# Two conversion steps kept out of the way of a fence copy, and one transfer issued earlier

## The chip, the core and the metric

The kernel runs on one core of a Trainium2 chip. A core has a matrix engine (TensorE, PE in the profile; PEld is its weight load), a vector engine (VectorE, DVE), a scalar engine (ScalarE, ACT), GpSimd (POOL) and SyncE (SP), which here only issues DMA transfers. Each engine works through its own list of instructions; semaphores make one wait for another. The metric is the device time of one execution in microseconds, the median of several runs. Less is better.

## The reference

A retention block feeds a feed-forward block. For each of 8 batches and 8 heads the first computes decayed scores and multiplies them with v; its output, laid out as 4608 tokens by 512 features, goes through a feed-forward layer with a squared relu and 2048 hidden features.

```python
scores = scale * np.matmul(q, k.transpose(0, 1, 3, 2))        # q, k, v: (8, 8, 576, 64) float32
Dmat = np.where(rel >= 0, gamma[:, None, None] ** rel[None, :, :], 0.0)
attn = np.matmul(scores * Dmat[None, :, :, :], v)
x = attn.transpose(0, 2, 1, 3).reshape(B * S, H * D)          # (4608, 512)
h = np.maximum(x @ w_in, 0.0)                                 # w_in: (512, 2048) float64
out = (h * h @ w_out).astype(np.float32)                      # w_out: (2048, 512) float64
```

The weights arrive in double precision. The kernel turns them into float32 on the chip with integer operations on their bits.

## The kernel before

The work runs in two phases. In the first, the retention runs over chunks of 128 tokens and the first half of the feed-forward layer (x times w_in, relu, square; the result is called g) runs between its parts, block by block of 512 tokens. g is stored to DRAM. In the second phase g is loaded again and multiplied with w_out. The matrix products of blocks 1 to 8, and those of the second phase, use a scheme with seven products in place of eight, so that sums of operands are made on VectorE.

One chunk of the retention has three parts that write the same two banks of PSUM ("x's banks"). Between the second and the third stands a copy on ScalarE that reads one column of both banks and whose value is never used. It is the fence: the third part's matmuls write these banks and so wait for the copy, and the copy waits for the second part's.

```python
def retain_b(i):                       # the state of earlier chunks times q
    ...
            nc.tensor.matmul(x_at(hp, b, h), lhsT=u[rows(e), hp, :], rhs=...)                # L455
    nc.scalar.copy(u_sb[(2 * ci + (cs // CH)) % 3][:, 0:2, 0:1], xp[0][:, :, cs - CH:cs - CH + 1])   # L458

def retain_c(i):                       # scores times v, within the chunk (matmuls: L420)
    ...
```

The order of a chunk from the fifth on; `turn` transposes q and k, `scores` makes the scores, `ffn(i, half)` runs steps of the feed-forward block:

```python
retain_a(i - 1)
if i < N_CH: turn(i)
ffn(i - 1, 0)
retain_b(i - 1)                        # ends with the fence copy
if i < N_CH: scores(i)
retain_c(i - 1)
ffn(i - 1, 1)
```

A piece of a weight is converted in steps. Two of them run on ScalarE, as a pair, on 128x512 elements:

```python
def beside():
    nc.scalar.activation(exp, exp, AF.Relu, bias=exp_bias[:, 0:1], scale=2.0 ** 23)   # L213
    nc.scalar.activation(frac, lo, AF.Copy, scale=2.0 ** -52)                         # L214
```

Steps `one` (L205), `two` (L209), `three` (L217), `four` (L220) and `five` (L223) are VectorE's. The pieces of w_in are converted during the first block (`convert(6)` takes six of these steps, one piece). Those of w_out are converted during the later blocks: each step of a block (`ffn_in`) takes one part from the generator `w_out_parts`, in which `two` and `beside` are one part; sums and stores to DRAM follow the pieces.

In the first block a step is `first_in`: four matmuls (L541) and a relu of their result on ScalarE (L545), then a square on VectorE (L548). `ffn` before the change:

```python
def ffn(i, half):
    gone[0] += ...
    if steps and steps[0][0] == 0:     # the first block
        step()
        convert(6)
        if half and steps and steps[0][0] == 0:
            step()
            convert(6)
        return
    ...                                # want: where the blocks should stand by now
    if steps:
        step()
    while steps and done[0] < int(want):
        step()
```

In the later blocks a step is `ffn_in`: four matmuls (L576) and the evacuation of a bank by ScalarE (L586, L592) or VectorE (L588 to L602).

The last block's steps run after the retention has ended; between them the loads of the second phase are issued:

```python
while steps:
    n, f, *args = steps[0]
    if n == N_BLK - 1:
        if n_last in (0, 5, 10):
            fetch_g(n_last // 5)               # transfers 0, 1, 2 of g
        if n_last in (2, 9, 16, 23):
            fetch_w2(2 + n_last // 7)          # converted w_out, 1792 KB each
        ...
        n_last += 1
    step()
some(len(queue))
fetch_w2(NP - 1)
fetch_g(3)                                     # transfer 3 of g, 1024 KB
for k in range(N_K + 1):                       # the second phase, matmuls: L800
    ...
    fetch_g(k + 4)
```

Transfers 0 to 3 go to four buffers of their own (`a`), 4 and 5 to parts of a buffer that the first phase uses (`room`).

Of the kernel before, what the change touches and what calls it, by code (L numbers as in the profile page):

```python
# [40 lines left out]
def kernel(  # L41
# [147 lines left out]
    def fetch_w(j):  # L189
        if j < len(pieces) and wide:  # L190
            nc.sync.dma_start(raw_of(j).bitcast(I64).rearrange("p (c f) -> p c f", c=N_DM), piece_src(j))
# [4 lines left out]
    def round_parts(j):  # L196
        words = raw_of(j).bitcast(U32).rearrange("p (n two) -> p n two", two=2)
        lo, hi = words[:, :, 0], words[:, :, 1]
        frac = raw_of(j).rearrange("p (n two) -> p n two", two=2)[:, :, 0]
        exp = exp_of(j).bitcast(U32)  # L200
        t = piece_dst(j)
        bits = t.bitcast(U32)

        def one():
            nc.vector.tensor_scalar(exp, hi, 20, 0x7FF, op0=ALU.logical_shift_right, op1=ALU.bitwise_and)  # L205

        def two():

            nc.vector.tensor_scalar(bits, as_dst(j, hi), 0xFFFFF, 0x100000, op0=ALU.bitwise_and, op1=ALU.bitwise_or)  # L209
# [6 lines that stand above are left out]
        def three():  # L216
            nc.vector.scalar_tensor_tensor(t, bits, 2.0 ** -20, as_dst(j, frac), op0=ALU.mult, op1=ALU.add)  # L217

        def four():
            nc.vector.tensor_tensor(t, t, as_dst(j, exp_of(j)), op=ALU.mult)  # L220

        def five():
            nc.vector.scalar_tensor_tensor(bits, as_dst(j, hi), 0x80000000, bits, op0=ALU.bitwise_and, op1=ALU.bitwise_or)  # L223

        if not wide:
            to = t if pieces[j][0] == 0 else t.rearrange("p o s f -> p (o s) f")
            return [lambda: nc.sync.dma_start(to, piece_src(j))] + [lambda: None] * 5
        return [one, two, beside, three, four, five]
# [16 lines left out]
    def w_out_parts():  # L245

        for j in range(N_W1, N_W1 + 3):
            yield lambda j=j: fetch_w(j)
        for j in range(N_W1, len(pieces)):
            one, two, beside, three, four, five = round_parts(j)  # L250
            yield one
            yield lambda two=two, beside=beside: (two(), beside())
            yield three
            yield four

            def last(j=j, five=five):
                five()
                fetch_w(j + 3)

            yield last  # L260
            wi, m, e = pieces[j]
            mh, mq = divmod(m, N_MQ)
            if e == 1:

                at = slice(2 * mh, 2 * mh + 2)
                b = [stage[0][:, o, at, :] for o in range(4)] + [stage[1][:, o, at, :] for o in range(3)]
                r1, r2, r3, r4 = right_sums(*b)
                yield lambda r1=r1, r2=r2: (r1(), r2())
                yield lambda r3=r3, r4=r4: (r3(), r4())
            if e == 1 and mh == 1:  # L270

                for st_, at in ((stage[0], slice(0, 4)), (stage[1], slice(4, 7))):
                    yield from right_sums(*(st_[:, :, o, :] for o in range(NP)))
                    yield lambda st_=st_, at=at, mq=mq: nc.sync.dma_start(
                        w2_dram[at, :, mq, :].rearrange("o p f -> p o f"), st_.rearrange("p o s f -> p o (s f)"))
# [33 lines left out]
    def convert(count):  # L309
        for _ in range(count):  # L310
            f = next(w_in_steps, None)
            f and f()
# [197 lines left out]
    def g_of(mp):  # L510
        return {name: g_room[mp % 2][:, s, :, :] for s, name in enumerate(G_ORDER)}
# [16 lines left out]
    def some(count=1):  # L528
        for f in queue[:count]:
            f and f()  # L530
        del queue[:count]
# [29 lines left out]
    def ffn_in(n, mp, j):  # L561

        if j == 0 and mp == 0:

            if n not in sums_x:
                sums_x[n] = sum_x(n)
            for f in sums_x[n]:
                f()
        left, right, to = PRODUCTS[j]
        if j in OPENS:  # L570
            sums[to] = ps_f.tile([128, 2, HT], F32, tag="f", name=f"h_{to}")
        p = sums[to]
        for mm in range(2):
            w = w_in[mp][:, mm, WI_SLOT[left], :, :]
            for c in range(2):
                nc.tensor.matmul(p[:, mm, :], lhsT=w[:, c, :], rhs=xs[n][right][:, c, :],  # L576
                                 start=(j in OPENS and mm == 0 and c == 0), stop=(j in CLOSES and c == 1),
                                 skip_group_check=True)
        g = g_of(mp)
        p1, u2, p15 = (p_room[mp % 2][:, s, :, :] for s in range(3))  # L580

        def square(t):
            nc.vector.scalar_tensor_tensor(t, t, 0.0, t, op0=ALU.max, op1=ALU.mult)  # L583

        if j == 0:
            nc.scalar.copy(p1, p)  # L586
        elif j == 1:
            nc.vector.tensor_tensor(u2, p, p1, op=ALU.add)  # L588
        elif j == 2:
            nc.vector.tensor_tensor(p15, p, p1, op=ALU.add)  # L590
        elif j == 3:
            nc.scalar.activation(g["A11"], p, AF.Relu)  # L592
            nc.gpsimd.tensor_tensor(g["A11"], g["A11"], g["A11"], op=ALU.mult)  # L593
        elif j == 4:
            nc.vector.tensor_tensor(g["A22"], p, p15, op=ALU.add)  # L595
            square(g["A22"])
        elif j == 5:

            nc.vector.tensor_tensor(g["S3"], p, u2, op=ALU.add)
            square(g["S3"])  # L600
        else:
            nc.vector.tensor_tensor(g["A12"], p, p1, op=ALU.add)  # L602
            square(g["A12"])
            queue.extend(g_sums(n, mp))

        if mp == N_MP - 1 and j in (3, 4, 5) and n_next[0] > n + 1:
            if n + 1 not in sums_x:
                sums_x[n + 1] = sum_x(n + 1)
            sums_x[n + 1].pop(0)()
        if j in (6, 0, 1, 2, 3):  # L610
            some(2 if n == 1 and mp == 0 else 1)
        if n == 1 and 1 <= j < 5 and mp + 1 < N_MP:
            sums_w.setdefault(mp + 1, sum_w_in(mp + 1)).pop(0)()

        if n >= 3 or n_w2[0] < 3 + 2 * 5:
            n_w2[0] += 1
            f = next(w_out_steps, None)
            f and f()
            if n == N_BLK - 2 and (mp, j) in ((2, 3), (3, 3)):
                assert f is None  # L620
                fetch_w2(mp - 2)

    steps = []
    w_out_steps = w_out_parts()
    n_w2 = [0]

    def block_steps(n):
# [4 lines left out]
    def step():  # L634
        n, f, *args = steps.pop(0)
        done[0] += 1
        f(*args)
# [9 lines left out]
    done = [0]  # L647
# [3 lines left out]
    def ffn(i, half):  # L651

        gone[0] += chunks[max(0, min(i, N_CH - 1))][3] / 2
        if steps and steps[0][0] == 0:
            step()
            convert(6)
            if half and steps and steps[0][0] == 0:
                step()
                convert(6)
            return  # L660
        if not behind:
            behind.append((gone[0] - HALF, done[0]))
        points = behind + [p for p in PACE if p[0] > behind[0][0]]
        want = points[-1][1]
        for (x0, y0), (x1, y1) in zip(points, points[1:]):
            if gone[0] < x1:
                want = y0 + (y1 - y0) * (gone[0] - x0) / (x1 - x0)
                break
        if steps:
            step()  # L670
        while steps and done[0] < int(want):
            step()

    turn(0)
    for i in range(N_CH + 1):
# [57 lines left out]
    def fetch_g(k):  # L733
        if k < N_K:
            nc.sync.dma_start(A(k), g_dram[BLOCKS[k // NP], k % NP, :, :, :])
# [99 lines left out]
    n_last = 0  # L835
    while steps:
        n, f, *args = steps[0]
        if n == N_BLK - 1:
            if n_last in (0, 5, 10):
                fetch_g(n_last // 5)  # L840
            if n_last in (2, 9, 16, 23):
                fetch_w2(2 + n_last // 7)
            if n_last == N_MP * NP - 5:
                for f in inner_sums(0):
                    f()
            n_last += 1
        step()
    some(len(queue))
    fetch_w2(NP - 1)
    fetch_g(3)  # L850
    steps_0 = sums_0()
    for k in range(N_K + 1):
        assert k + 4 < N_K - NP or next(steps_0, None) is None
# [3 lines left out]
        for e in range(3):  # L857
# [8 lines left out]
            f = next(steps_0, None)  # L866
# [53 lines left out]
```

## Time and profile before

| | before |
|---|---|
| time, median of 3 runs | 1009.67 us (1004.35 to 1010.14) |
| span of the profiled execution | 1004.7 us |
| copies of L458 | 40, 133 to 168 ns each |
| L213, 128x512 | 32, 722 ns each (median) |
| L214, 128x512 | 32, 662 ns each (median) |
| transfers of g to `a` | 43, 1024 KB, 7.1 us from issue to landing (median) |

The page has the engines' busy shares and the span cut in 40 slices, in which a digit is the busy share of a slice in tenths:

```profile
## 2 busy tenths in 40 slices
PE   6999999999999999999999998999999999999998
...
DVE  1678797667878888798885776877677677777765
ACT  2344331122222222312311000000000000000000
...
DMA  8974665664786877579566989674764757556351
```

The first phase fills the first 24 slices or so, the second phase the rest. Other views list, for each engine, what it waited for and how long, and the instructions in order of time with the idle time ahead of each. A row such as "PE x L1 <- ACT y L2: 3.0, 5, 1.0" means that PE's instruction of line 1 was released by ScalarE's instruction of line 2 in 5 cases after 3.0 us of idle time in all, 1.0 us at the longest.

### The profile page before, as it was taken

How to read it: one execution, taken by the hardware profiler on the slowest of the kernel's cores; microseconds unless marked ns; L12 is line 12 of the kernel's file. 1: busy time of each engine (PE TensorE's matmuls, PEld its weight loads, DVE VectorE, ACT ScalarE, POOL GpSimd, SP SyncE). 2: the span in 40 equal slices, each digit the busy share in tenths (PEclk: the TensorE clock that was granted, in tenths of full speed). 3: DMA queues.
4: the chain of work that ended last, by engine and by line, in shares of the span. 5: the costliest groups of instructions: out<-in, count | busy, mean ns of one | idle time of the engine just before them, and what ended most of it. 6: DMA issues, size and time to landing. Idle time of an engine off the chain costs nothing.

```text
span 1004.7 us, 24101 instructions
## 1 busy us (share of the span) xinstructions
PE 975.3 (97%) x10376; PEld 862.4 (86%) x10376; DVE 749.7 (75%) x1418; ACT 188.9 (19%) x459; POOL 81.8 (8%) x82
## 2 busy tenths in 40 slices
PE   6999999999999999999999998999999999999998
PEld 4544688888888888788888888999999999999997
DVE  1678797667878888798885776877677677777765
ACT  2344331122222222312311000000000000000000
POOL 1200011011111111111021000000000000000000
PEclk9999999999999999999999999999999999999999
DMA  8974665664786877579566989674764757556351
GB/s 201 241 212 143 183 180 177 171 195 151 207 291 203 239 259 228 139 258 282 150 243 249 401 351 350 252 273 168 252 237 162 273 189 272 187 212 217 119 210 43
DMA packets 187658, 220.34 MB, mean 219 GB/s; under 512 B 119200, under 2 KB 137632, under 8 KB 178592
## 3 DMA queue, kind: packets, MB, share of 16 engines
q1 hardware_dynamic: 187552, 218.81, 66.8%
q8 instruction: 81, 1.33, 0.5%
q14 instruction: 25, 0.20, 0.1%
HBM read 129.39 MB, written 89.39 MB: 218 GB/s over the span
## 4 chain that ended last, share of the span: by engine, by line
PE 87%; DVE 7%; DMA 2%; ACT 2%; SPq 2%; issue 1%; DVEq 0%
PE o_b L800 16%; PE h_b L576 15%; PE o_c L800 11%; PE o_a L800 11%; PE h_a L576 10%; PE h_c L576 9%; PE h_ps L541 6%; PE x_ps L420 3%; PE t_ps L373 2%; PE x_ps L455 2%; DMA a<-g_dram 1%; PE sc_ps L399 1%; DVE room L583 1%; SPq L142 1%; DMA k_ld<-in_k_dram 1%
## 5 line engine op out<-in xcount | busy, mean ns | idle before, releaser
L576 PE MATMUL h_b<-room,w 128*128 128x256 f32 x736 | 177.3, 384 | 1.8 <-DVE room L504 1.2
L576 PEld LDWEIGHTS h_b<-room,w 128*128 128x128 f32 x736 | 137.1, 190 | 22.4 <-DVE room L595 1.4
L800 PE MATMUL o_b<-w,room 128*128 128x128 f32 x1168 | 144.5, 275 | 0.2 <-DVE room L751 0.2
L800 PEld LDWEIGHTS o_b<-w,room 128*128 128x128 f32 x1168 | 137.2, 192 | 0.5 <-DVE room L751 0.4
L800 PE MATMUL o_c<-w,room 128*128 128x128 f32 x1008 | 123.0, 275 | 0.0
L800 PEld LDWEIGHTS o_c<-w,room 128*128 128x128 f32 x1008 | 117.7, 192 | 0.0
L576 PE MATMUL h_c<-room,w 128*128 128x256 f32 x480 | 114.3, 381 | 0.0
L576 PE MATMUL h_a<-room,w 128*128 128x256 f32 x448 | 107.5, 383 | 0.0
L576 PEld LDWEIGHTS h_c<-room,w 128*128 128x128 f32 x480 | 90.5, 190 | 12.5
L576 PEld LDWEIGHTS h_a<-room,w 128*128 128x128 f32 x448 | 83.8, 190 | 11.8
L800 PE MATMUL o_a<-w,a 128*128 128x128 f32 x688 | 85.9, 275 | 2.7 <-DMA a<-g_dram 2.7
L800 PEld LDWEIGHTS o_a<-w,a 128*128 128x128 f32 x688 | 81.3, 192 | 2.9 <-issue 2.9
L593 POOL TENSOR_TENSOR room<-room 128x512 f32<-128x512 f32 x32 | 36.4, 1139 | 435.9 <-ACT room L592 380.7
L583 DVE SCALAR_TENSOR_TENSOR room<-room 128x512 f32<-128x512 f32 x96 | 67.4, 702 | 3.3
L811 ACT COPY r<-o_a 128x128 f32<-128x128 f32 x54 | 14.4, 266 | 276.9 <-PE o_a L800 246.3
L420 PEld LDWEIGHTS x_ps<-ret,v_ld 64*64 64x64 f32 x1152 | 42.5, 143 | 22.8 <-issue 14.1
L420 PE MATMUL x_ps<-ret,v_ld 64*64 64x64 f32 x1152 | 52.4, 234 | 9.1 <-ACT u_sb L458 9.1
L541 PE MATMUL h_ps<-room,w 128*128 128x512 f32 x128 | 59.9, 616 | 0.8 <-ACT room L477 0.7
L595 DVE TENSOR_TENSOR room<-h_b,room 128x512 f32<-128x512 f32 x32 | 22.0, 689 | 42.0 <-PE h_b L576 42.0
L408 POOL TENSOR_TENSOR v_ld<-v_ld,dv 128x512 f32<-128x512 f32 (+1 forms) x40 | 45.0, 1129 | 80.4 <-DMA v_ld<-in_v_dram 67.4
L541 PEld LDWEIGHTS h_ps<-room,w 128*128 128x128 f32 x128 | 24.0, 195 | 27.8 <-issue 25.2
L807 DVE TENSOR_TENSOR small<-o_b,small 128x128 f32<-128x128 f32 x63 | 18.3, 291 | 38.5 <-PE o_b L800 38.4
(94 smaller groups left out, 1369.4 us busy)
## 6 DMA issues: line engine op xcount, KB each, us to landing
g_dram<-room SPq DMA_DIRECT2D x32, 1792.0 KB, 8.1
a<-g_dram SPq DMA_DIRECT2D x43, 1024.0 KB, 7.1
room<-g_dram SPq DMA_DIRECT2D x20, 1024.0 KB, 6.0
w<-w_dram SPq DMA_DIRECT2D x7, 1792.0 KB, 12.1
out_dram<-room SPq DMA_DIRECT2D x18, 512.0 KB, 3.3
v_ld<-in_v_dram SPq DMA_DIRECT2D x32, 256.0 KB, 4.0
w<-in_moe_w_in_dram SPq DMA_DIRECT2D x16, 512.0 KB, 4.9
w<-in_moe_w_out_dram SPq DMA_DIRECT2D x16, 512.0 KB, 4.0
```

Source lines behind the costliest of these rows:

```text
L373: nc.tensor.transpose(p[:, h, j, hp, :], loaded[i][j][rows(h), 2 * hp:2 * hp + 2, :], ident[rows(h), rows(h)])
L408: nc.gpsimd.tensor_tensor(vs[:cs], vs[:cs], dv[:cs, :, ci:ci + 1].to_broadcast([cs, H, D]), op=ALU.mult)
L420: own.append(lambda hp=hp, e=e, b=b: nc.tensor.matmul(x_at(hp, b, h), lhsT=s["vs"][rows(h), 2 * hp + b, :], rhs=s["ret"][rows(h), e, hp, : ...
L455: nc.tensor.matmul(x_at(hp, b, h), lhsT=u[rows(e), hp, :], rhs=s["qT"][rows(e), hp, CH * h:CH * h + CH], start=clears(b, hp // 2), stop=Fa ...
L541: nc.tensor.matmul(p.rearrange("p h t -> p (h t)"), lhsT=w[:, c, :], rhs=xT[0][:, c, :], start=(c == 0), stop=(c == N_DM - 1))
L576: nc.tensor.matmul(p[:, mm, :], lhsT=w[:, c, :], rhs=xs[n][right][:, c, :], start=(j in OPENS and mm == 0 and c == 0), stop=(j in CLOSES a ...
L583: nc.vector.scalar_tensor_tensor(t, t, 0.0, t, op0=ALU.max, op1=ALU.mult)
L593: nc.gpsimd.tensor_tensor(g["A11"], g["A11"], g["A11"], op=ALU.mult)
L595: nc.vector.tensor_tensor(g["A22"], p, p15, op=ALU.add)
L800: nc.tensor.matmul(p, lhsT=s["lefts"][left][:, m, :], rhs=w_out[j][:, m, WO_SLOT[right], :], start=(i in OPENS and m == 0), stop=(i in CLO ...
L807: nc.vector.tensor_tensor(s["u2"], p, s["p1"], op=ALU.add)
L811: nc.scalar.copy(r[:, 0, 0:128], p)
```

## The change

Three things. In the first block, the first half of a chunk now runs its conversion ahead of its step, so that L213 and L214 come before the relu in ScalarE's order and not between the relu and the fence copy. In the later blocks, the last step before the fence does not take a part that holds the pair; the pair waits for the next step. And the fourth transfer of g is issued in the last block, at its sixteenth step, and no longer after it. The aim is that the fence copy finds ScalarE free, and that the fourth transfer lands before it is needed.

```diff
@@ w_out_parts
-            yield lambda two=two, beside=beside: (two(), beside())
+            yield two, beside
@@ ffn_in
         if n >= 3 or n_w2[0] < 3 + 2 * 5:
-            n_w2[0] += 1
-            f = next(w_out_steps, None)
-            f and f()
+            if not (held[0] and type(w_out_next[0]) is tuple):
+                n_w2[0] += 1
+                f = w_out_next[0]
+                w_out_next[0] = next(w_out_steps, None)
+                for f in f if type(f) is tuple else (f,):
+                    f and f()
@@ ffn
         if steps and steps[0][0] == 0:
-            step()
-            convert(6)
+
+            for f in (step, lambda: convert(6)) if half else (lambda: convert(6), step):
+                f()
@@ ffn, later blocks
-        if steps:
-            step()
-        while steps and done[0] < int(want):
-            step()
+        count = max(1, int(want) - done[0])
+        while steps and count:
+            held[0] = half == 0 and count == 1
+            step()
+            count -= 1
+        held[0] = False
@@ the last block
-            if n_last in (0, 5, 10):
+            if n_last in (0, 5, 10, 15):
                 fetch_g(n_last // 5)
@@ after it
     fetch_w2(NP - 1)
-    fetch_g(3)
```

Left out of the diff: the start values of `held` and `w_out_next`, and an assertion on the latter.

More of the change, by code (lines that the diff above doesn't have):

```diff
@@ L615, in ffn_in @@
         if n >= 3 or n_w2[0] < 3 + 2 * 5:
-            n_w2[0] += 1
-            f = next(w_out_steps, None)
-            f and f()
+            if not (held[0] and type(w_out_next[0]) is tuple):
[4 more added lines that the diff above has]
+                    f and f()
             if n == N_BLK - 2 and (mp, j) in ((2, 3), (3, 3)):
-                assert f is None
+                assert w_out_next[0] is None
                 fetch_w2(mp - 2)
@@ L626 @@
     w_out_steps = w_out_parts()
+    w_out_next = [next(w_out_steps)]
+    held = [False]
     n_w2 = [0]
```

## The prediction

> **What bounds the kernel now.** I read the page's busy shares first, then the list of what TensorE waited for, then the timeline around the longest of those waits.
>
> ```profile
> span 1004.7 us, 24101 instructions
> PE 975.3 (97%) x10376; PEld 862.4 (86%) x10376; DVE 749.7 (75%) x1418; ACT 188.9 (19%) x459; POOL 81.8 (8%) x82
> ```
>
> TensorE (PE) is busy 975.3 us of 1004.7; no other engine is near. The change neither adds nor removes a matmul, so 975.3 stays, and all that can be won lies in 1004.7 - 975.3 = 29.4 us. The list of PE's waits (engine, line, whom it waited for: us in total, times, longest) says whose they are:
>
> ```profile
> PE x_ps L420 <- ACT u_sb L458: 9.1, 13, 1.4
> PE t_ps L373 <- DMA k_ld<-in_k_dram: 4.4, 4, 3.2
> PE o_a L800 <- DMA a<-g_dram: 2.7, 1, 2.7
> PE sc_ps L399 <- DVE qT L381: 2.0, 1, 2.0
> PE x_ps L455 <- ACT u_sb L429: 2.0, 4, 0.5
> PE h_b L576 <- DVE room L504: 1.2, 1, 1.2
> ```
>
> The first and the third row are the targets: the copy of L458 holds PE back 13 times, and one transfer of g once. The rest of the 29.4 us is the first loads, the ends of the program and small waits, which nothing in the diff touches.
>
> One wait of the first kind, from the timeline (start, length, instruction, in brackets the idle time before it); ScalarE, then PE:
>
> ```profile
> 65.05 0.60 ACT L545 ACTIVATE room<-h_ps 128x512 f32<-128x512 f32 x1 [2.38 <-PE h_ps L541]
> 65.55 0.71 ACT L213 ACTIVATE w<-w,exp_bias 128x512 uint32<-128x512 uint32 x1
> 66.16 0.64 ACT L214 ACTIVATE w<-w 128x512 f32<-128x512 uint32 x1
> 66.70 0.15 ACT L458 COPY u_sb<-x_ps 128x2 f32<-128x2 f32 x1
> ```
> ```profile
> 65.23 0.65 PE L399 MATMUL sc_ps<-qT,kT 64*64 64x64 f32 x32
> 66.90 0.27 PE L420 MATMUL x_ps<-ret,v_ld 64*64 64x64 f32 x2 [1.03 <-ACT u_sb L458]
> ```
>
> The copy itself takes 0.15 us. It is late because two conversion steps (L213, L214) stand in front of it in ScalarE's order, behind a relu that had to wait for the projection. PE has only the scores (0.65 us) to hide it under, then idles 1.03 us.
>
> **What the Trainium skill says.** Its page "PSUM — Partial Sum Buffer", section "Engine vs sequencer instructions", says that ScalarE's queue is strictly first in, first out. The lines above agree: the copy's input was there once L455 had ended at about 65.4, and it ran at 66.70, after both conversions. "ScalarE: Activation LUTs", section "What ACT_TABLE_LOAD costs", gives 280 ns + 0.833 ns per element with a pointer bias and 186 ns + 0.833 ns with immediates: 707 and 613 ns for 512 elements, with 93 ns of overlap. The trace has medians of 722 ns (L213) and 662 ns (L214); I use those, about 1.3 us for the pair. For the transfer, "DMA: Bandwidth & Descriptors", section "Queues, rings and completion order", says each DMA engine consumes its descriptors in ring order; the landings below agree.
>
> **Part 1: the first block, four chunks.** In the first half of a chunk `convert(6)` now precedes `step()`. ScalarE's order becomes L213, L214, relu, fence copy instead of relu, L213, L214, fence copy. The pair needs no matmul: its exponents were extracted by the previous call, and it runs while PE is still in the projection, where ScalarE stood idle 2.38 us. The relu then ends at the same 65.65 and the copy near 65.75; PE finished the scores at 65.88. So the wait goes to nothing. The four are idle times in the timeline at 52.37, 66.90, 81.60 and 96.15: 1.06 + 1.03 + 0.81 + 0.81 = 3.71 us. VectorE's order moves too: a square that stood ahead of five conversion steps now follows them, about 5 x 0.6 = 3 us later. It feeds only a store to g, so nothing on PE waits for it.
>
> **Part 2: the conversion of w_out.** In the last step before the fence a piece's pair is withheld and taken by the next step. The waits concerned lie at 323.83, 375.70, 403.61 and 416.26: 0.33 + 1.42 + 1.32 + 0.82 = 3.89 us. In the built order of the changed kernel three of these copies still have L213 and L214 directly before them: the one at 249, which cost PE nothing before; the one at 416, where the pair now belongs to a step two earlier (3.8 us of matmuls lie between); and, new, the one at 462, with one step of 1.92 us between and a pair of 1.3 us. I count all 3.89. The price: each withheld pair moves the rest of the w_out chain one slot later; by its end that is four slots. A slot is one FFN step with its share of attention: seven blocks of 28 steps between 116.7 and 547.9, 2.2 us each. So the last store of converted w_out, issued at 525.1, goes to about 534. The first re-load of w_out was issued at 533.3 and is needed by the first L800 matmul at about 602, so even 12 us of delay stay hidden.
>
> What remains of the 9.1 us: four copies in the first 35 us (4 x 0.28, another branch of the code) and the last one at 546.12 (0.37, no scores behind it), 1.5 us. 3.71 + 3.89 = 7.60 us is the share removed.
>
> **Part 3: the fourth transfer of g.**
>
> ```profile
> 606.83 0.51 SPq L492 DMA_DIRECT2D w<-w_dram  x1
> 607.40 1.13 SPq L735 DMA_DIRECT2D a<-g_dram  x1
> 608.58 3.40 SPq L771 DMA_DIRECT2D g<-g_dram  x3
> 613.60 0.80 SPq L735 DMA_DIRECT2D room<-g_dram  x2
> ```
> ```profile
> 607.40 14.12 DMA a<-g_dram
> ```
> ```profile
> 621.65 1.13 PE L800 MATMUL o_a<-w,a 128*128 128x128 f32 x8 [2.71 <-DMA a<-g_dram]
> 626.55 0.69 DVE L750 TENSOR_TENSOR room<-room 128x512 f32<-128x512 f32 x1 [0.79 <-DMA room<-g_dram]
> ```
>
> The first fence is SyncE's own timeline, the second a piece of the chain of waits, the third PE and VectorE. The transfer is issued behind 1.8 MB of weights and lands 14.12 us later; PE waits 2.71 us. In the changed order it is issued after the store of 572.6 and before the weights of 578.1; that store landed at 585.3, so in ring order it lands by about 590, 25 us before its use, and delays the weights behind it by 3 us, which are used after 620. But the wait could pass to the next transfer, `room<-g_dram`, which also lands only just in time: VectorE waited 0.79 us for it at 626.55. It is issued at 613.60 whatever happens, because it needs the landing of the last store of g. With 1 MB less ahead of it in the rings it lands earlier by 1 MB at the 367 GB/s moved between 606 and 630, 2.9 us, while PE arrives 2.7 us earlier: the two shifts cancel, VectorE's small wait stays, and PE, whose first matmul on it ran at 627.98 for a landing near 626.5, has over 1 us to spare. I take 2.5 of the 2.71 us.
>
> **Sum.** 3.71 + 3.89 + 2.5 = 10.1 us. VectorE is at 93.1 of 114 us between 318 and 432, and its order shifts by up to four slots there; PE already waits for it twice at such places (L504 1.2 us, L595 0.5 us). For new ones of this kind I take off 0.4. That leaves 9.7 us.
>
> **Rivals.** (a) *VectorE takes the wait over.* Withheld steps pile conversion work on a later step, an evacuation comes late, and a PSUM bank is not free. For it: those two rows, and 82% load. Against: the sum of its work is unchanged, and a withheld step moves only 0.4 us of it. It would give back 1 to 3 us: about 1002. (b) *The transfer's wait moves on to the next one.* For it: the 0.79 us. Against: the landing order. It would give back up to 2.5 us: about 1002. (c) *SyncE blocks.* The stores of w_out, later by four slots, now directly precede the re-load that must wait for them, and SyncE issues in order; a store of g behind them could come late and hold the ScalarE relu that needs its buffer (one such row exists: ScalarE waited 5.0 us for a store of g). PE would lose 1 to 3 us. (d) *The conversion steps are not what delays the copy*: with the copy still held by the relu, part 1 would bring only half. Against it: the relu ends at 65.65.
>
> **Range and chances.** The three times are 1004.35, 1009.67 and 1010.14; their median is the base, though a lower true middle is as likely, so I put the result a little under 1009.67 - 9.7 = 1000.0: 999.3 us. The spread of the runs (about 3 us to each side) and of the sum (2 us) give 994.5 to 1004. Two per cent is 20.2 us, twice the waits that the change can reach at all, so faster by over 2% needs a lucky median: 0.02. Slower by over 2% needs a mechanism that nothing shows: 0.01. Within: 0.97.
>
> **What would show it.** The row `x_ps L420 <- ACT u_sb L458` falls from 9.1 us in 13 to about 1.5 in 5; the row for `o_a` on `a<-g_dram` is gone; the waits of PE on VectorE stay under 3 us in sum; PE's busy time is 975 within 1 and the span about 995. It is wrong if these rows vanish and the span does not follow (then idle time of PE was not what set the end), if a row of PE waiting for VectorE or for `room<-g_dram` of 2 us or more appears, or if L458 keeps more than 4 us.

## The result and the profile after

| | before | after |
|---|---|---|
| time, median of the runs made together | 1008.9 us (4 runs, 1004.35 to 1010.14) | 995.26 us (4 runs, 993.57 to 997.33) |
| span of the profiled execution | 1004.7 us | 995.6 us |
| ratio of the times | | 0.9874, 95% interval 0.9834 to 0.9913 |

The kernel is 12.7 us faster by the times (1 - 0.9874 = 1.26% of 1008.9), and 9.1 us by the two profiled spans. The busy time of the engines, from the page of the changed kernel:

```profile
span 995.6 us, 24088 instructions
PE 973.7 (98%) x10376; PEld 861.8 (87%) x10376; DVE 748.0 (75%) x1418; ACT 189.7 (19%) x459; POOL 81.2 (8%) x82
```

As many matmuls as before, and PE still the only engine near its span. Its busy time is 1.6 us lower for the same work. By itself this shows nothing, for three more executions of the changed kernel had 971.4 to 974.6. But in the later blocks (defined below) PE was busy 481.2 us before and 480.5 after, in all four executions of the changed kernel; that will matter. The list of PE's waits in the changed kernel (us in total, times, longest):

```profile
PE t_ps L373 <- DMA k_ld<-in_k_dram: 6.6, 5, 3.3
PE x_ps L420 <- ACT u_sb L458: 2.5, 6, 1.0
PE x_ps L455 <- ACT u_sb L429: 2.0, 4, 0.5
PE sc_ps L399 <- DVE qT L381: 1.8, 1, 1.8
PE h_b L576 <- DVE room L504: 0.9, 1, 0.9
...
PE h_b L576 <- DVE room L595: 0.6, 1, 0.6
```

The fence row fell from 9.1 us in 13 to 2.5 in 6, and the row for the transfer of g is gone. The first loads (`k_ld`) cost 2.2 us more in this execution, from 4.4 to 6.6; they lie in the first 33 us, where nothing of the change stands. Three more executions of the changed kernel had 6.5 to 6.8, and its variants below 4.5 to 5.9.

One fence of the first block, the one that the prediction showed at 66.70, now (ScalarE, then PE):

```profile
63.68 0.67 ACT L214 ACTIVATE w<-w 128x512 f32<-128x512 uint32 x1
65.70 0.60 ACT L545 ACTIVATE room<-h_ps 128x512 f32<-128x512 f32 x1 [1.35 <-PE h_ps L541]
66.20 0.16 ACT L458 COPY u_sb<-x_ps 128x2 f32<-128x2 f32 x1
```
```profile
65.89 0.69 PE L399 MATMUL sc_ps<-qT,kT 64*64 64x64 f32 x32
66.41 0.26 PE L420 MATMUL x_ps<-ret,v_ld 64*64 64x64 f32 x1
```

The pair is done before the projection is; the copy follows the relu at once and is over at 66.36, while the scores still run. L420 carries no idle time. It even starts 0.17 us before the scores' shown end (65.89 + 0.69 = 66.58), because PE's matmuls are pipelined and the profile models their ends.

**Where the time came from.** The list of one line's instructions gives the first and the last start of its matmuls. Three such starts cut the span into stages: the first L541 begins the first block, the first L576 the later blocks, the first `o_a` the second phase. Before, then after (durations min/median/max in ns, then first and last start in us):

```profile
L541 PE MATMUL h_ps<-room,w x128: 592/592/1219, 36.4 to 113.4; 128*128 128x512 f32 x128
L576 PE MATMUL h_a<-room,w x448: 379/379/484, 114.6 to 596.7; 128*128 128x256 f32 x150
L800 PE MATMUL o_a<-w,a x688: 273/275/348, 602.1 to 996.8; 128*128 128x128 f32 x172
```
```profile
L541 PE MATMUL h_ps<-room,w x128: 592/592/1219, 38.0 to 111.1; 128*128 128x512 f32 x128
L576 PE MATMUL h_a<-room,w x448: 379/379/483, 112.3 to 590.5; 128*128 128x256 f32 x150
L808 PE MATMUL o_a<-w,a x688: 273/275/275, 595.9 to 987.7; 128*128 128x128 f32 x172
```

The first block went from 114.6 - 36.4 = 78.2 us to 74.3, the later blocks from 487.5 to 483.6, the second phase from 1004.7 - 602.1 = 402.6 to 399.7. That is 3.9 + 3.9 + 2.9 = 10.7 us; the stretch ahead of the first block took 1.6 us more (36.4 to 38.0), which leaves the 9.1 us of the spans. The same cut of every kernel of this study is the table that the rest leans on, since a stage repeats from run to run far better than a span does (us; four executions of the changed kernel gave 483.6 for the middle one, 399.6 or 399.7 for the last and 74.2 to 74.8 for the first):

| kernel | first block | later blocks | second phase |
|---|---|---|---|
| before | 78.2 | 487.5 | 402.6 |
| part 1 alone | 74.4 | 487.5 | 405.8 |
| part 2 alone | 78.2 | 483.6 | 403.8 |
| part 3 alone | 78.5 | 487.5 | 399.7 |
| all three (the change) | 74.3 | 483.6 | 399.7 |
| before, two issues swapped | 78.3 | 487.5 | 402.5 |
| change, transfer ten steps later | 74.2 | 483.6 | 400.5 |
| change, long fence | 76.1 | 494.2 | 399.9 |
| change, fence on VectorE | 92.6 | 518.5 | 399.7 |
| change, pair withheld two steps | 74.2 | 484.9 | 399.7 |
| change, two steps at the border only | 75.4 | 481.8 | 399.7 |

**The one wait that came new.** The fence row has 2.5 us where 1.5 were to be left. The rest is a single wait of 0.98 us. ScalarE, VectorE and PE around it, in the changed kernel:

```profile
495.36 0.72 ACT L213 ACTIVATE w<-w,exp_bias 128x512 uint32<-128x512 uint32 x1 [4.96 <-DVE w L205]
495.99 0.66 ACT L214 ACTIVATE w<-w 128x512 f32<-128x512 uint32 x1
496.55 0.58 ACT L592 ACTIVATE room<-h_a 128x512 f32<-128x512 f32 x1
497.02 0.15 ACT L458 COPY u_sb<-x_ps 128x2 f32<-128x2 f32 x1
```
```profile
491.30 0.69 DVE L506 TENSOR_TENSOR room<-room 128x512 f32<-128x512 f32 x1
...
494.30 0.68 DVE L519 TENSOR_TENSOR room<-room 128x512 f32<-128x512 f32 x1
494.90 0.42 DVE L205 TENSOR_SCALAR w<-w 128x512 uint32<-128x512 uint32 x1
```
```profile
495.60 0.65 PE L399 MATMUL sc_ps<-qT,kT 64*64 64x64 f32 x32
497.23 0.27 PE L420 MATMUL x_ps<-ret,v_ld 64*64 64x64 f32 x2 [0.98 <-ACT u_sb L458]
```

Here the pair belongs to the last step but one before the fence, so nothing withholds it. It should have run long before. But its input L205 stands in VectorE's order behind a row of sums without a gap (the border of two blocks: L503 to L506 and L517 to L519), and came at 494.90. ScalarE stood idle for 4.96 us, then ran the pair, an evacuation and the copy, and PE had finished its scores at 496.25.

This is the 37th of the 40 fences. Before the change it stood at 502.37, and its pair had run 10 us ahead of it, so that it cost nothing:

```profile
492.28 0.72 ACT L213 ACTIVATE w<-w,exp_bias 128x512 uint32<-128x512 uint32 x1 [3.67 <-DVE w L205]
...
502.37 0.16 ACT L458 COPY u_sb<-x_ps 128x2 f32<-128x2 f32 x1
```

It is the last pair of the chain of w_out. Each pair withheld earlier has moved the chain one step later, and so this pair to within 1.7 us of its fence.

### The profile page after: what moved, and what is told of

It is laid out like the page before. It is cut to its first block, busy times and chain, and to the rows that moved or that the text cites. A ratio compares the mean times of both kernels' runs of the same rounds, so it can differ in the third digit from the quotient of the medians.

```text
span 995.6 us, 24088 instructions
## 1 busy us (share of the span) xinstructions
PE 973.7 (98%) x10376; PEld 861.8 (87%) x10376; DVE 748.0 (75%) x1418; ACT 189.7 (19%) x459; POOL 81.2 (8%) x82
## 4 chain that ended last, share of the span: by engine, by line
PE 90%; DVE 5%; SPq 2%; DMA 1%; ACT 1%; issue 1%; DVEq 0%; ACTq 0%
PE o_b L808 17%; PE h_b L576 16%; PE o_c L808 11%; PE o_a L808 11%; PE h_c L576 10%; PE h_a L576 10%; PE h_ps L541 5%; PE x_ps L420 3%; PE t_ps L373 2%; PE x_ps L455 2%; PE sc_ps L399 2%; SPq L142 1%; DVE room L583 1%; DMA k_ld<-in_k_dram 1%; PE u_ps L423 1%
## 5 line engine op out<-in xcount | busy, mean ns | idle before, releaser
L576 PE MATMUL h_b<-room,w 128*128 128x256 f32 x736 | 177.2, 383 | 1.6 <-DVE room L504 0.9
L576 PEld LDWEIGHTS h_b<-room,w 128*128 128x128 f32 x736 | 137.2, 190 | 21.8 <-PE t_ps L373 1.1
L576 PE MATMUL h_c<-room,w 128*128 128x256 f32 x480 | 114.3, 381 | 0.0
L576 PE MATMUL h_a<-room,w 128*128 128x256 f32 x448 | 107.5, 383 | 0.0
L576 PEld LDWEIGHTS h_c<-room,w 128*128 128x128 f32 x480 | 90.5, 190 | 12.5
L576 PEld LDWEIGHTS h_a<-room,w 128*128 128x128 f32 x448 | 83.8, 190 | 11.8
L541 PE MATMUL h_ps<-room,w 128*128 128x512 f32 x128 | 59.9, 617 | 0.9 <-ACT room L477 0.7
L420 PEld LDWEIGHTS x_ps<-ret,v_ld 64*64 64x64 f32 x1152 | 42.1, 142 | 15.2 <-issue 11.5
L420 PE MATMUL x_ps<-ret,v_ld 64*64 64x64 f32 x1152 | 51.9, 233 | 2.5 <-ACT u_sb L458 2.5
L595 DVE TENSOR_TENSOR room<-h_b,room 128x512 f32<-128x512 f32 x32 | 22.1, 690 | 41.3 <-PE h_b L576 41.3
L381 DVE TENSOR_TENSOR qT<-t_ps,dq 128x512 f32<-128x512 f32 (+1 forms) x40 | 25.3, 633 | 31.4 <-ACT kT L379 20.9
L541 PEld LDWEIGHTS h_ps<-room,w 128*128 128x128 f32 x128 | 24.0, 195 | 28.1 <-issue 26.0
## 6 DMA issues: line engine op xcount, KB each, us to landing
w<-w_dram SPq DMA_DIRECT2D x7, 1792.0 KB, 12.9
```

Source lines behind the costliest of these rows:

```text
L381: nc.vector.tensor_tensor(to, p[:, :n_h, j, :, :], dq[:, :, c0:c0 + cs].rearrange("p d (h t) -> p h d t", h=n_h), op=ALU.mult)
L420: own.append(lambda hp=hp, e=e, b=b: nc.tensor.matmul(x_at(hp, b, h), lhsT=s["vs"][rows(h), 2 * hp + b, :], rhs=s["ret"][rows(h), e, hp, : ...
L541: nc.tensor.matmul(p.rearrange("p h t -> p (h t)"), lhsT=w[:, c, :], rhs=xT[0][:, c, :], start=(c == 0), stop=(c == N_DM - 1))
```

## The experiments

**Each part by itself.** The three parts, each alone on the kernel before, and the changed kernel with them.

Part 1 alone:

```diff
-            step()
-            convert(6)
+            for f in (step, lambda: convert(6)) if half else (lambda: convert(6), step):
+                f()
```

> Part 1 alone: the kernel before, with the conversion ahead of the step in the first half of a chunk in the first block. Theory (the pair L213 and L214 is all that makes these four fence copies late): the four waits of 1.06, 1.03, 0.81 and 0.81 us go, the row of PE waiting for L458 falls from 9.1 to about 5.4 us in 9 cases, the stretch from the first to the last L541 falls from 77.0 to about 73.3 us, and the time by 3.7 us (ratio 0.996). Rival (the relu of L545 holds the copy as well): only about half of it goes, the row stays above 7 us, the time falls by 2 us at most.

Part 2 alone (`held`, and the pair as a part of its own that can wait, as in the change):

```diff
-            yield lambda two=two, beside=beside: (two(), beside())
+            yield two, beside
...
+            held[0] = half == 0 and count == 1
```

> Part 2 alone: the kernel before, with the pair withheld in the last step before the fence in the later blocks. Theory: the waits of 0.33, 1.42, 1.32 and 0.82 us go, but the one new wait that the changed kernel shows near 496 us (0.98 us, the pair made late by VectorE and not by its place) comes with it: the row of PE waiting for L458 is about 6.2 us, the stretch of the L576 matmuls falls by 2.9 to 3.9 us, and so does the time (ratio 0.996 to 0.997). Rival (the new wait belongs to part 1 or to chance): the row falls to 5.2 us. Second rival (the four slots' delay of the w_out chain costs something): PE's waits for VectorE or for stores grow by 1 us or more.

Part 3 alone:

```diff
-            if n_last in (0, 5, 10):
+            if n_last in (0, 5, 10, 15):
...
-    fetch_g(3)
```

> Part 3 alone: the kernel before, with the fourth transfer of g issued at the sixteenth step of the last block. Theory: PE's wait of 2.7 us for it is gone, VectorE waits for the next transfer (room<-g_dram) some 2 us where it waited 0.8, PE does not wait for it at all, and the second phase (first to last L800) falls from 397.4 to about 394.6 us; the time falls by 2.7 us (ratio 0.997). Rival (the wait passes to the next transfer): PE gets a wait of 1 to 2.5 us on room<-g_dram or on sums of it, and the time hardly falls.

The whole change, measured beside them:

> The changed kernel once more, beside its three parts on one chip. If the waits of TensorE are all that the change moves, its gain is the sum of the parts' gains, about 10 us (3.7 + 3.3 + 2.8), ratio 0.990. If the parts help or hinder each other, or if something that is no wait of PE gives the 13.6 us seen between the medians, the gain is over 12 us here too while the parts add up to 10.

| | time, us | runs | ratio to before, 95% interval | saved |
|---|---|---|---|---|
| part 1 | 1005.56 | 17 | 0.9967 (0.9954 to 0.9980) | 3.3 |
| part 2 | 1003.51 | 6 | 0.9951 (0.9933 to 0.9969) | 4.9 |
| part 3 | 1005.69 | 12 | 0.9965 (0.9954 to 0.9977) | 3.5 |
| all | 995.58 | 4 | 0.9873 (0.9852 to 0.9894) | 12.8 |

The base of the last column is 1008.71 us, the median of 28 runs of the kernel before. The three parts alone add up to 11.7 us, within the interval of the whole (10.7 to 14.9), so nothing shows that they get in each other's way. Both are above the 10 us that the waits alone would give; the section on the prediction comes back to this. The fence rows of part 1 alone and of part 2 alone, and PE's waits on g with part 1 alone:

```profile
PE x_ps L420 <- ACT u_sb L458: 5.4, 9, 1.4
PE o_a L801 <- DMA a<-g_dram: 3.1, 1, 3.1
```
```profile
PE x_ps L420 <- ACT u_sb L458: 5.9, 10, 1.0
...
PE o_a L807 <- DMA a<-g_dram: 2.4, 1, 2.4
```

9.1 - 5.4 = 3.7: exactly the four waits that part 1 was to remove, all of them. Rival (d), that the relu holds the copy just as long, falls. Part 2 has the new wait of 0.98 us already (at 498.2 in its trace), so it comes from withholding and not from part 1 or 3. In the table of stages each part shortens its own stage and leaves the others, with one exception: the second phase of parts 1 and 2 alone is 3.2 and 1.2 us *longer* than before. The last section tells why.

**Does the order of two issues do as much as the earlier place?** The kernel before, with the transfer of g put ahead of the weights at the end of the last block:

```diff
-    fetch_w2(NP - 1)
     fetch_g(3)
+    fetch_w2(NP - 1)
```

> The kernel before, with the last two issues after the last block exchanged: the fourth transfer of g first, the last 1792 KB of w_out second. Theory (what made the transfer late is mainly the data ahead of it in the rings): it lands 4 to 5 us earlier, near 617, and PE's wait of 2.7 us for it is gone although it is issued only about 0.5 us earlier; the weights are used only from about 640 on and can wait. Rival (it is late because it is issued late): it lands within 1 us of before and PE still waits 2 us or more.

One run: 1006.66 us beside 1007.42 of the kernel before, and the second phase took 402.5 us in place of 402.6. The transfer landed at 617.6 and PE's wait on it was gone. In its place (PE, then VectorE):

```profile
627.52 1.16 PE L800 MATMUL o_a<-w,room 128*128 128x128 f32 x8 [1.93 <-DMA room<-g_dram]
```
```profile
627.50 0.69 DVE L750 TENSOR_TENSOR room<-room 128x512 f32<-128x512 f32 x1 [5.08 <-DMA room<-g_dram]
```

The wait moved to the next transfer, as rival (b) had it for the change itself. As many bytes stand in the same rings before that transfer as did before; whichever is served first, the last one needed comes late (near 626.5 before, at 627.5 here). So part 3 wins because 1 MB leaves the crowded stretch, not because one transfer is preferred.

**Is the sixteenth step a special place?** The changed kernel, with the transfer ten steps later:

```diff
-            if n_last in (0, 5, 10, 15):
-                fetch_g(n_last // 5)
+            if n_last in (0, 5, 10, 25):
+                fetch_g(min(3, n_last // 5))
```

> The changed kernel with the fourth transfer of g issued at the twenty-sixth step of the last block in place of the sixteenth, after the sixth load of w_out. Theory (any place ahead of the last store of g and the last load of w_out will do): it lands before 608 us, PE does not wait for it, and the span is that of the changed kernel within its start-up luck. Rival (the sixteenth step matters, later places collide with the stores of g at the end of the block): PE waits 1 us or more for it, or for room<-g_dram.

One run, 996.54 us. The transfer was issued at 592.1 and landed at 601.3, PE did not wait, and VectorE waited 3.0 us for `room<-g_dram` instead of 2.0. The second phase is 0.8 us longer. This one later place, still before the crowd, is nearly as good.

**What does a fence cost that is longer by 0.4 us?** The changed kernel with a copy of 512 columns (256 in the first and last chunk of a batch) in place of the two, 0.59 us (0.37) for 0.16; its value is still unused:

```diff
-        nc.scalar.copy(u_sb[(2 * ci + (cs // CH)) % 3][:, 0:2, 0:1], xp[0][:, :, cs - CH:cs - CH + 1])
+        lo = 0 if ci else cs - CH
+        seen = xp[0][:, :, 0:256].rearrange("p a (g t) -> p a g t", g=2)[:, :, :, lo:cs]
+        nc.scalar.copy(f_sb[:, :, :, lo:cs], seen)
```

> The changed kernel with a longer fence copy: it reads all columns of x's banks written so far (128x512 in the middle chunks of a batch, 128x256 in the first and last) in place of 128x2, so it takes about 0.58 or 0.37 us in place of 0.16. Theory (the copy lies under the scores with some 0.18 us to spare, and what goes beyond is lost by PE one for one): the row of PE waiting for the fence grows from 2.5 us in 6 cases to about 10 us in 30 or so, and the span by about 7.8 us. Rival (ScalarE is busy 19% and has room, PE goes on with other work): the row and the span stay within 1.5 us.

One run, 1010.21 us, span 1008.5 us. Its fence row:

```profile
PE x_ps L421 <- ACT f_sb L461: 11.4, 30, 1.4
```

The number of waits is as expected (30) and their sum nearly (11.4 for about 10). The span is another matter: the row grew by 8.9 us, the span by 12.9. PE's *busy* time makes up for it, in the later blocks 484.6 us for 480.5, with the same matmuls. An unhindered L420 starts while the scores drain, as seen above at 66.41; one that has waited starts after them, so the overlap is lost and the loss is booked as busy time. The Trainium skill's page "TensorE: Matmul & The Clock Gate", section "Single matmul latency", gives a single warm bf16 matmul about 166 ns of latency that is not its streaming; the overlap here, 0.17 us, is of that size, though these matmuls are float32 and its end is modelled, and no run shows that it is the same thing. Over the first block and the later blocks PE's busy time grew by 5.0 us for 24 more waits, about 0.2 us each. The new wait of the changed kernel gives the cost directly, once a run without it is at hand (the last experiment).

**Would VectorE be a better place for the fence?** The changed kernel with the copy on VectorE:

```diff
-        nc.scalar.copy(u_sb[...][:, 0:2, 0:1], xp[0][:, :, cs - CH:cs - CH + 1])
+        nc.vector.tensor_copy(u_sb[...][:, 0:2, 0:1], xp[0][:, :, cs - CH:cs - CH + 1])
```

> The changed kernel with the fence copy on VectorE in place of ScalarE, same columns. Theory (a fence is as late as the queue of its engine, not as its own length): VectorE runs up to 3.7 us behind at these places, so 25 or so of the 35 fences from the fifth chunk on come late and PE loses 25 to 42 us. Rival (a copy this short costs nothing anywhere): the span stays within 2 us.

One run, 1052.51 us:

```profile
PE x_ps L420 <- DVE u_sb L458: 44.4, 30, 3.5
```

The copy takes the same time (155 ns) but stands behind whatever VectorE has in its list. 44.4 us is a little above the range; the span is 55 us longer, which again is more than the row, partly by lost overlap and partly because the TensorE clock fell in the first block (0.91 on average, 0.98 to 1.00 in the changed kernel). A fence of the same length thus costs far more behind a fuller queue; the experiment before this one shows that its own length counts too.

**Withhold the pair for two steps?** The idea against the new wait, with the parts made up later two at a time, so that the chain of w_out does not fall behind (`take_w_out` takes one part):

```diff
-            held[0] = half == 0 and count == 1
+            held[0] = half == 0 and count <= 2
...
+            if held[0] and pair:
+                owed[0] += n >= 3
+            else:
+                take_w_out()
+                if owed[0] and not pair and type(w_out_next[0]) is not tuple:
+                    owed[0] -= 1
+                    take_w_out()
```

> The changed kernel with two edits: the pair is withheld in the last two steps before the fence, and a step after a withheld one takes two parts (never the pair) until the w_out chain has caught up. Theory (the new wait of 0.98 us at the 37th fence comes from VectorE, 3 us behind at a block's border, which makes the exponents late, so that the pair of the last step but one still runs in front of the fence): the wait goes, the row falls from 2.5 us in 6 cases to 1.5 us in 5, the stretch of the L576 matmuls falls by 1.1 us (0.98 and some 0.15 that a wait costs beyond the idle time shown), and the time falls by about 1 us against the changed kernel, not more than the runs can just tell. Rival (the catching up puts more on VectorE in single steps): PE's rows for VectorE grow by as much, and nothing is won.

Beside it the changed kernel again:

> The changed kernel, on the chip of the next run and as its measure: ratio to the kernel before about 0.987, PE's row for the fence 2.5 us in 6 cases.

998.04 us (5 runs; ratio to before 0.9900, 0.9882 to 0.9918) against 998.06 (4 runs; 0.9887, 0.9869 to 0.9906): no gain.

```profile
PE sc_ps L399 <- DVE qT L381: 2.7, 2, 1.9
...
PE h_b L576 <- DVE room L504: 1.7, 1, 1.7
PE x_ps L420 <- ACT u_sb L458: 1.5, 5, 0.4
PE h_b L576 <- DVE room L595: 1.1, 2, 0.5
```

The fence row is at 1.5 in 5 as hoped. But VectorE, which now gets two parts in one step, is late elsewhere: L504 0.9 to 1.7, L595 0.6 to 1.1, and a new wait of 0.86 us for `qT`. The later blocks took 484.9 us for 483.6. Here rival (a) of the prediction is real.

**Withhold it only at the border, and make nothing up.** In the first seven steps of a block, among which VectorE makes the border's sums, the pair is now withheld in the last two steps before the fence and not in the last alone (the expectation counts the step that takes the pair as well, and says three for two; its "first softmax-block end" is the end of the first block); the second transfer of w_out starts three steps later to go with it. `steps[0][3]` is the group of seven within the block:

```diff
-            held[0] = half == 0 and count == 1
+            held[0] = half == 0 and count <= (2 if steps[0][3] == 0 else 1)
...
-            if n == N_BLK - 2 and (mp, j) in ((2, 3), (3, 3)):
+            if n == N_BLK - 2 and (mp, j) in ((2, 6), (3, 3)):
```

> The changed kernel with one edit: in the step whose last-but-one step crosses a block border (the one in which VectorE has the border sums to make), the pair L213/L214 is withheld for three steps instead of two, and the second transfer of w_out is started that much later. Theory: PE's one new wait of about 1.0 us for that fence copy (at 496 us in the trace of the changed kernel) comes from the pair of the step at the border, which is released late because VectorE is busy with the border sums; then this wait is gone, the fence row falls from 2.5 us in 6 to about 1.5 us in 5, the stage between the first softmax-block end and the second phase is 1.0 us shorter (483.6 to about 482.6), and the time about 1 us shorter than that of the changed kernel, 994.3 where that one has 995.3. Rival: the copy is late for another reason (ScalarE's own queue), or the pairs moved later load VectorE at the next border; then the fence row keeps 6 waits, or PE's waits for VectorE (L504, L595) and for qT grow from 3.3 us together by about as much as is won, and the stage stays at 483.6 or grows.

Beside it:

> The changed kernel itself, as the measure for the run beside it: 995 to 998 us, fence row 2.5 us in 6, the middle stage 483.6 us.

The same place in this run (ScalarE, then PE), and its fence row and that of L504:

```profile
496.41 0.60 ACT L592 ACTIVATE room<-h_a 128x512 f32<-128x512 f32 x1 [4.84 <-PE h_a L576]
497.02 0.16 ACT L458 COPY u_sb<-x_ps 128x2 f32<-128x2 f32 x1
```
```profile
496.77 0.65 PE L399 MATMUL sc_ps<-qT,kT 64*64 64x64 f32 x32
497.24 0.27 PE L420 MATMUL x_ps<-ret,v_ld 64*64 64x64 f32 x2
```
```profile
PE x_ps L420 <- ACT u_sb L458: 1.5, 5, 0.4
...
PE h_b L576 <- DVE room L504: 0.3, 1, 0.3
```

The pair is out of the way and the wait is gone, as it was with the pair withheld for two steps everywhere. So the pair in front of the copy is shown as the cause; that VectorE's sums made it late is read from the timeline above. From the scores' start to L420's start it is 0.47 us here; in the changed kernel it was 497.23 - 495.60 = 1.63. The wait had thus cost 1.16 us where its row said 0.98. The later blocks took 481.8 us for 483.6: 1.8 saved, 1.2 by this fence and 0.6 by the row of L504. By the times, 995.72 us (4 runs; 0.9869, 0.9850 to 0.9888) against 996.99 for the changed kernel beside it (6 runs; 0.9883, 0.9865 to 0.9900). The intervals overlap, so that it is faster than the changed kernel is shown by the stage and only likely by the time. Its profiled span is not shorter (995.6 for 995.1): its start and first block, where the two programs are the same, took 2.2 us more (L576 first at 114.1 for 111.9).

## Why the prediction was right, and where it was not

*The time.* 999.3 was predicted and 995.26 measured, inside the range. The base was taken a little high (1009.67; 28 later runs have 1008.71), and the saving too low: 9.7 against 12.7 by the times (12.8, 11.4 and 11.8 in the three later comparisons) and 10.7 by the stages.

*Part 1, 3.71 us.* Right in place and number: all four waits went (the row to 5.4 with this part alone), and the copy ended at 66.36, with the relu about as predicted. The first block is 3.9 us shorter.

*Part 2, "I count all 3.89".* This is the step that failed, in its list of the copies that would still have a pair in front of them. The four waits named did go, and 3.89 was right for them. The three copies listed, at 249, 416 and 462 of the trace of before, are at 247, 409 and 456 in the changed kernel, and PE waits for none of them, as predicted. But the list holds only copies with a pair "directly before them", and leaves out the one of 502, where an evacuation (L592) stands between pair and copy. The four slots of delay were held against the deadline of the re-load alone, and not against the fences that a later pair would meet. Nor would the distance of one step have given it away: the pair at 462 had as much and was done 1.0 us ahead of its copy, while at the 37th fence VectorE's sums at the border of two blocks delayed the input. So 0.98 us came back, and the row kept 2.5 us in 6 and not 1.5 in 5. Withholding this pair as well removed the wait.

*Part 3, 2.5 of 2.71 us.* Right: the row is gone, and PE did not wait for the next transfer. VectorE's wait for that one was to stay at 0.8 us and grew to 2.0, so the two shifts did not quite cancel, but PE had time to spare. The transfer was issued at 566.8, just behind a store, and landed at 581.5, 14.7 us later, well before its use. Since PE lost nothing to the next transfer, the full amount came: 2.9 us by the stage.

```profile
566.38 0.37 SPq L521 DMA_DIRECT2D g_dram<-room  x1
566.80 0.56 SPq L743 DMA_DIRECT2D a<-g_dram  x1
```

*The sum.* The predicted rows shrank by 9.1 - 2.5 = 6.6 and 2.7, together 9.3 us; the stages by 10.7. The term that was mis-sized is the price of one wait: I took the idle time of the row, but a wait also costs the overlap of two groups of matmuls, and nine waits went for one that came. The 1.4 us over eight waits are 0.17 us each. This sits in PE's busy time, which I expected to stay "975.3" and which in the later blocks fell from 481.2 to 480.5. For the same reason 1004.7 - 975.3 was no strict bound for what could be won. That the 9.7 us come so near to the 10.7 is partly luck: a wait that was not seen (1.2 us too much) stands against the price of the waits and the 0.4 us taken off (too little). That the times fell by 12.7 and the stages by 10.7 lies within the uncertainty of the ratio, though all four comparisons of the times are above 10.7; the profile of before was also taken in an execution of 1006.41 us, on the quick side of its runs.

*The 0.4 us set aside for VectorE* were not used: L504 fell from 1.2 to 0.9 and L595 went from 0.5 to 0.6. The sign "under 3 us in sum" for PE's waits on VectorE was set wrong, as they were 3.9 us before (2.0 of it for `qT`) and 3.5 after.

*The rivals.* (a) VectorE takes the wait over: not by the change, but as soon as parts are made up two at a time. (b) the wait moves to the next transfer: not by the change, but when only the order is swapped. (c) SyncE blocks: ScalarE's wait for stores of g grew from 5.0 us in one case to 9.6 in two, but PE has no row of that kind. (d) the relu holds the copy: refuted by part 1 alone.

## What to carry to other kernels

A tiny copy that other engines wait for is as late as the longest thing that its engine can meet in front of it, so look not only at what stands before it in the order, but at when that is released; a busy engine two steps away can put it there. When work is put off, look at every fence that it can now meet, down to the end of its chain. The late transfer in the saturated stretch was mended here by moving its bytes out of the stretch, and not by changing the order within it. Price a wait of TensorE at its idle time plus the lost overlap, here about 0.2 us, and measure small gains by the lengths of stages, which here repeated to within 0.1 us in the later blocks where the times spread over 4 us.

## What the hardware did that was not expected

With parts 1 and 2 alone, which both keep the wait for the transfer of g, the second phase was longer than before. The windows show why. With part 1 alone, then with part 2 alone (a stretch and its length, busy us of PE, PEld, VectorE, ScalarE and GpSimd with instructions in brackets, then the granted TensorE clock, the DMA share and GB/s):

```profile
616.00:620.00 4.00, 1.39 (x13) 1.20 (x11) 0.00 (x0) 0.27 (x1) 0.00 (x0) 0.95 0.92 334
620.00:622.00 2.00, 1.53 (x7) 1.56 (x8) 1.64 (x5) 0.00 (x0) 0.00 (x0) 0.50 1.00 397
...
624.00:626.00 2.00, 2.00 (x12) 2.00 (x11) 0.47 (x2) 0.00 (x0) 0.00 (x0) 0.50 1.00 422
```
```profile
617.00:620.00 3.00, 2.86 (x13) 2.89 (x14) 2.94 (x7) 0.27 (x1) 0.00 (x0) 0.50 1.05 396
620.00:624.00 4.00, 4.00 (x37) 4.00 (x36) 3.02 (x9) 0.00 (x0) 0.00 (x0) 0.97 1.01 428
```

After an idle time of 3.08 us the clock was 0.50 for 6.8 us, after one of 2.42 us for 3.4 us, and the second phase came out 3.2 and 1.2 us longer. In finer windows the clock fell 2.2 and 2.1 us after PE's last matmul, while PE still waited. Yet the profile of before, idle for 2.71 us at the same place, shows a clock of 1.00 throughout, as does the swapped kernel with 1.93, so a fixed delay of that length is not the rule; what decides is not shown. One wait of some 2.5 us may thus cost up to twice its length, or not. The Trainium skill's page "TensorE: Matmul & The Clock Gate", section "Part 1: The HAM clock gate (the "warmup" mystery)", says that the clock halves after at least one idle window of about 3.4 us. The halving is seen, and the two slow stretches are about two and one times 3.4 us long; but no idle time of that length was needed, as 2.42 us were enough here. Part 3 removes this risk with the wait, which may be why the times fell by more than the two spans; no run tests that. The profiled execution of part 1 was the slowest of its 17 runs (1008.07 us for a median of 1005.56), so most runs may have been spared.
